# Pooled attention and a routed two-layer network: values products and normalizing of two chunks in halves of heads, an expert index ahead of a fold, one load held for another, and a new table of priorities

## The chip, the cores and the metric

The kernel runs on one core of one Trainium2 chip. The metric is the device time of one execution in microseconds (us), as the median of several runs. Before the change three runs gave 199.23, 200.05 and 202.09 us; their median is 200.05 us.

## What is computed

Eight batches, eight heads, 576 rows, head size 64. Keys and values are averaged over groups of eight rows (72 groups a head), attention runs over these, and its 4608 x 512 output goes through a router that picks one expert of eight for each row and through that expert's two-layer network.

```python
k_p = k.reshape(B, H, Sp, 8, D).mean(axis=3);  v_p = v.reshape(B, H, Sp, 8, D).mean(axis=3)
attn = softmax(scale * q @ k_p.T);             x = (attn @ v_p) as [4608, 512]
expert_idx = argmax(xn @ en.T / tau);          gate_w = softmax(...)[expert_idx]
out[mask_e] = gate_w * (relu(x[mask_e] @ w1[e]) @ w2[e])
```

## The kernel before

The eight batches are eight periods of work that overlap: while TensorE (PE) does the network of batch b, the attention of batch b+1 is put between its products. For each batch the kernel guesses one expert from the mean of the values and loads that expert's two weights; a block behind a branch at the end does a batch again if a row chose another expert.

The kernel is written as named steps, each with an engine, an assumed duration, a priority and the steps it waits for. A planner (`Plan.order`, line 135) runs them once through a model of the engines and the DMA wires, and the order that comes out is the order in which the instructions are written to the engines' queues. Every engine then works its queue strictly in order. The table `TUNED` adds numbers to the priorities, and so sets the order; `LOADS` fixes the order of the loads on GpSimd's queue (POOL); `BEHIND` says which store waits for which load. Where the planner expects PE to be idle in the first part, it writes filler products of ones (`keep_warm`, line 819) into PE's queue; their results are not used.

Names of steps, with the batch as the first number:

- V, K, Q: loads of values, keys and queries (POOL, lines 319 and 325). Batch 0's are cut in two (V0.0, V0.1, K0.0, K0.1, Q0.0, Q0.1). W1b, W2b: the two weights (lines 343 and 349; W10 is the first weight of batch 0). PKb: POOL reads the index of the guessed expert (line 359) and can then issue the weights.
- GM, GC, GL, GD, GE: mean of the values, its copy, its product with the expert embeddings, the maximum and its index on VectorE (DVE, lines 523 and 524), and the one-hot of it.
- VA, VB, KA, KB: folds of values and keys on DVE (line 448 and lines 455, 462); batch 0's keys are summed by PE (line 472). QT: transposes of the queries on DVE (line 548). KT, KE: the keys' transpose on PE and its copy.
- SC, EX: scores on PE (line 589) and exponentials on ScalarE (ACT, line 597), in two halves of the query columns (0 to 269 and 270 to 575 in batch 0), in two-bank PSUM tiles `pa` of which there are two.
- PV, XM, XT, XE, SQ: values product of a chunk of 128 rows (PE, line 634), its division by the row sum (DVE: a reciprocal on line 369 and a product on line 370), its transpose (PE, line 378), the copy of that, the sum of squares. There are five chunks a batch. In batch 0 chunks 0 and 1 need only the first half of the columns and use two PSUM tiles of one bank each, with heads 0 to 3 and 4 to 7.
- H, HE: the first layer in 16 pieces (line 709) and its relu (ACT or DVE, lines 715 and 717). Y, YL, YE, ST: the second layer in four chunks and a last half (lines 721 and 728), its scaling by the gate (line 734 or 736) and the store (SyncE's queue, SP).
- RT, RE, NA to ND: router and gate. PR, PP, PX: the test at the end of whether the branch is taken (lines 867 to 893).

What the diff touches: `store` and `note` (lines 333 to 340), `normalize` (line 364), the loads in `attention` (lines 417 to 436), VA of batch 0 (line 489), the loop over the chunks (lines 625 to 668) and `presence` (line 895 and its call on line 990).

Of the kernel before, what the change touches and what calls it, by code (L numbers as in the profile page):

```python
# [213 lines left out]
def kernel(  # L214
# [24 lines left out]
    NC = 5  # L239
# [854 lines left out]
```

## Time and profile before

| | |
|---|---|
| median of 3 runs | 200.05 us (199.23 to 202.09) |
| the profiled execution | 200.91 us |
| its span, first to last instruction | 199.1 us |
| PE busy | 188.6 us (95%), of this 15.7 us filler products |
| DVE, ACT, POOL busy | 139.8, 136.3, 43.0 us |
| mean granted TensorE clock | 0.993 |
| moved by DMA | 38.71 MB, mean 194 GB/s |

The profile is of one execution. Busy time of PE is from the start of a product to its modelled end, and consecutive products overlap; so PE can be shown busy where it is slowed by something else. POOL's rows for DMA are the time of issuing, the landing is counted separately.

### The profile page before, as it was taken

Reading aid. Unit: us, or ns where it says so; the run is one execution under the profiler, and the core shown is the slowest. Engines: PE = TensorE matmul, PEld = TensorE weight load, DVE = VectorE, ACT = ScalarE, POOL = GpSimd, SP = SyncE. Lnnn points to the kernel's source line nnn. Section 1 sums busy time; section 2 is a strip of 40 time slices with the busy share of each in tenths; the row PEclk is TensorE's granted clock in tenths of the full one; section 3 lists DMA queues with packets and bytes.
Section 4 is the critical chain, followed back from the end, with each engine's and each line's share of the span. In section 5 each row is a group of like instructions: output and inputs, shape, how many; then the busy total and the mean of one; then the engine's idle time right before and its main releaser. Section 6 shows DMA issues by size and latency. Waiting matters only on the chain.

```text
span 199.1 us, 5342 instructions
## 1 busy us (share of the span) xinstructions
PE 188.6 (95%) x2080; PEld 123.8 (62%) x2081; DVE 139.8 (70%) x409; ACT 136.3 (68%) x313; POOL 43.0 (22%) x59
## 2 busy tenths in 40 slices
PE   7969999999999999999999999999999999999980
PEld 5754787547864676468666566567665677568540
DVE  1274799659996996678997997878998559322610
ACT  4017886768896979759966779459976988558440
POOL 7443025232204321025102500043000510002000
PEclk9999999999999999999999999999999999999997
DMA  3999999999999999999999999999996699992042
GB/s 46 185 197 185 206 210 192 205 193 205 212 182 189 215 208 201 213 206 232 246 172 214 186 233 247 215 204 230 254 219 199 182 213 212 233 317 71 3 176 71
DMA packets 27839, 38.71 MB, mean 194 GB/s; under 512 B 4248, under 2 KB 14488, under 8 KB 27808
## 3 DMA queue, kind: packets, MB, share of 16 engines
q0 software_dynamic: 21904, 28.85, 86.7%
q1 hardware_dynamic: 5824, 9.39, 13.9%
q8 instruction: 18, 0.29, 0.6%
q14 instruction: 13, 0.11, 0.2%
q10 hardware_dynamic: 80, 0.07, 0.1%
HBM read 61.88 MB, written 9.44 MB: 358 GB/s over the span
## 4 chain that ended last, share of the span: by engine, by line
PE 80%; DVE 8%; DMA 4%; issue 2%; ACT 1%; POOL 1%; DVEq 0%; ACTq 0%; POOLq 0%
PE pb L709 27%; PE pb L721 22%; PE pa L589 6%; PE pa L709 5%; DMA kr<-in_k_dram 4%; PE pa L721 3%; DVE x L370 3%; PE pa L634 3%; PE pb L378 3%; PE pb L821 2%; PE pb L728 2%; PE pb L387 2%; DVE r_all L369 1%; DVE qT L548 1%; PE pb L472 1%
## 5 line engine op out<-in xcount | busy, mean ns | idle before, releaser
L709 PE MATMUL pb<-xt,w 128*128 128x288 f16 (+2 forms) x432 | 61.3, 287 | 0.0
L709 PEld LDWEIGHTS <-w 128*128 128x128 f16 x512 | 47.1, 98 | 15.1 <-issue 4.6
L721 PE MATMUL pb<-w,hT 128*128 128x512 f16 x224 | 52.7, 379 | 0.0
L597 ACT ACTIVATE at<-pa 72x576 f16<-72x576 f32 (+2 forms) x64 | 38.2, 642 | 3.9 <-PE pa L589 3.5
L721 PEld LDWEIGHTS <-hT 128*128 128x128 f16 x256 | 23.2, 98 | 24.9 <-issue 1.3
L655 ACT ACTIVATE sq<-x 128x512 f16<-128x512 f16 x40 | 25.2, 631 | 13.8 <-DVE x L370 8.8
L715 ACT ACTIVATE hT<-pb 128x288 f16<-128x288 f32 (+2 forms) x74 | 28.6, 411 | 5.4 <-PE pb L709 3.3
L734 ACT ACTIVATE y<-pb,gm_all 128x512 f32<-128x512 f32 (+1 forms) x29 | 18.5, 639 | 14.0 <-PE pb L721 10.9
L370 DVE TENSOR_TENSOR x<-pa,r_all 128x512 f16<-128x512 f32 x38 | 26.3, 692 | 2.1
L548 DVE STREAM_TRANSPOSE qT<-qq 128x576 f16<-128x576 f16 x32 | 23.2, 754 | 0.4 <-DMA qq<-in_q_dram 0.4
L398 POOL TENSOR_TENSOR ssq_all<-ssq_all,half_c 128x5 f32<-128x5 f32 x8 | 10.4, 1294 | 50.8 <-ACT sq L655 50.8
L349 POOL DMA_DIRECT2D w<-in_moe_w_dram x8 | 5.5, 688 | 64.3 <-PE pb L728 17.0
L717 DVE TENSOR_SCALAR hT<-pb 128x288 f16<-128x288 f32 (+2 forms) x34 | 14.8, 447 | 6.5 <-PE pb L709 6.2
L448 DVE TENSOR_TENSOR vr<-vr 72x2048 f16<-72x2048 f16 (+1 forms) x16 | 15.1, 941 | 3.3 <-DMA vr<-in_v_dram 3.3
L821 PE MATMUL pb<-ones_m 128*128 128x256 f16 x102 | 15.7, 297 | 1.5 <-DVE half_c L828 1.5
L589 PE MATMUL pa<-qT,kpT 32*72 32x288 f16 (+2 forms) x256 | 15.6, 294 | 0.0
L378 PEld LDWEIGHTS <-x 128*128 128x128 f16 x160 | 10.9, 98 | 6.3 <-DVE x L370 2.3
L378 PE MATMUL pb<-ident_h,x 128*128 128x128 f16 x144 | 13.7, 220 | 1.0 <-DVE x L370 0.7
L634 PEld LDWEIGHTS <-at 72*128 72x128 f16 x320 | 13.1, 98 | 1.9 <-issue 0.3
L634 PE MATMUL pa<-vpx,at 72*128 72x65 f16 x304 | 14.2, 194 | 0.0
L448 DVE TENSOR_TENSOR kr<-kr 72x2048 f16<-72x2048 f16 (+1 forms) x14 | 13.2, 942 | 0.3 <-DMA kr<-in_k_dram 0.3
L650 ACT COPY xt<-pb 128x512 f16<-128x512 f16 (+1 forms) x25 | 13.0, 538 | 0.5 <-PE pb L378 0.3
(116 smaller groups left out, 197.1 us busy)
## 6 DMA issues: line engine op xcount, KB each, us to landing
w<-in_moe_w_dram POOLq DMA_DIRECT2D x16, 1024.0 KB, 16.5
out_dram<-y SPq DMA_DIRECT2D x32, 256.0 KB, 5.9
vr<-in_v_dram POOLq DMA_DIRECT2D x7, 576.0 KB, 21.0
kr<-in_k_dram POOLq DMA_DIRECT2D x7, 576.0 KB, 17.6
qq<-in_q_dram POOLq DMA_DIRECT2D x7, 576.0 KB, 16.0
out_dram<-y SPq DMA_DIRECT2D x15, 64.0 KB, 7.0
qq<-in_q_dram POOLq DMA_DIRECT2D x2, 288.0 KB, 8.9
vr<-in_v_dram POOLq DMA_DIRECT2D x1, 512.0 KB
```

Of the source, the lines that this page charges most:

```text
L370: nc.vector.tensor_tensor(out=x[:, ts(i, np_)], in0=pxv[:, :, 1:129].rearrange("p a (r d) -> p a r d", d=D), in1=rv.unsqueeze(3).to_broadc ...
L378: nc.tensor.transpose(out=pt.bitcast(FP16)[:, ts(w, 128)], in_=xf[:, ts(w, 128)], identity=ident_h)
L448: nc.vector.tensor_tensor(out=t[:, :, 0:m], in0=t[:, :, 0:m], in1=t[:, :, m:2 * m], op=ALU.add)
L548: nc.vector.transpose(out=qT.tile[:, a].rearrange("p t c e -> p (t c e)")[:, cols], in_=qq.tile[:, a, cols]),
L589: nc.tensor.matmul(out=tiles[m // 2].tile[0:gs, m % 2 * 512:m % 2 * 512 + (p1 - p0) * T], lhsT=kpT.tile[ts(m, R), a, c, 0:gs], rhs=qT.tile ...
L597: nc.scalar.activation(out=t.tile[:, :, p0 * T:p1 * T].rearrange("g r (p t) -> g r p t", t=T), in_=p.tile[0:G].rearrange("g (r c) -> g r c ...
L634: nc.tensor.matmul(out=px[h // 2 // np_].tile[:, o:o + 65], lhsT=at[h // 2].tile[:, h % 2, c0:c0 + 128], rhs=vp.tile[:, h // 2, 1 + h % 2 ...
L655: nc.scalar.activation(out=sq, in_=x.tile.rearrange("p a r d -> p (a r d)"), func=AF.Square, accum_out=ssq_all[:, b, c:c + 1])
L709: nc.tensor.matmul(out=p[:, 0:c1 - c0], lhsT=w1v[:, kk, w // 2, w % 2, :], rhs=xt[:, kk, c0:c1], start=(kk == 0), stop=(kk == 3))
L715: nc.scalar.activation(out=dst, in_=src, func=AF.Relu)
L721: landing[f"Y{c}"] = nc.tensor.matmul(out=p, lhsT=hT[w][:, ts(c, 128)], rhs=w2[:, w // 2, w % 2, :], start=(w == 0), stop=(w == 7))
L821: nc.tensor.matmul(out=p[:, 256:512], lhsT=ones_m[:, 0:128], rhs=ones_m[:, 0:256], start=True, stop=True)
```

## The change

1. `LOADS` is reordered. On POOL's queue V1 is no longer issued right behind Q0.1, it comes behind PK0, and it waits in addition until K0.1 has landed (`wait_for`). K2 goes ahead of PK1, V2 behind it, and the later loads are reordered too. The planner's assumed delays of K0.1 and Q0 change.
2. In batch 0 the fold VA waits for GD (the index) and no longer for GC, so the index is written ahead of the fold on DVE.
3. In chunks 0 and 1 of batch 0 PV and XM are two steps each, one for each half of the heads (names PV0.0.0, PV0.0.1 and so on). A half waits only for the exponentials of its own heads. The instructions are the same in number: before, the step already issued one reciprocal and one product for each of the two PSUM tiles.
4. `presence` gets a later base for its priority.
5. `TUNED` is another table, so the order of nearly everything differs. PE's queue has 114 fillers, 103 before; the other instructions are the same in kind and number on every engine, but for one relu more on ACT and one fewer on DVE.

```diff
 TUNED = {
-    "GM5": 79.1, "Y1.0": 28.3, "RT7": 37.3, "SC6.1.1": -29.8, "VA7": 104.9, "H3.4.0": -54.3,
...
+    "Y2.3": 90, "YL4": 232.5, "PV5.2": -222.7, "PV1.3": 117.9, "H6.5.1": 29.6, "H0.4.1":
...
 LOADS = """
-V0.0 V0.1 K0.0 K0.1 Q0.0 Q0.1 V1 PK0 W10 K1 Q1.0 W20 V2 PK1 W11 K2 Q2.0 V3 W21 V4 K3 PK2 W12
...
+V0.0 V0.1 K0.0 K0.1 Q0.0 Q0.1 PK0 V1 W10 K1 Q1.0 W20 K2 PK1 V2 W11 Q2.0 V3 W21 PK2 W12 K3
...
+    def wait_for(ins, name):
+        tc.add_manual_dep(ins, landing[name], mybir.DependencyInfo(
+            mybir.DependencyClass.Sync, mybir.DependencyReason.DATA), reason="late transfer")
+
     def note(name, load):
         landing[name] = load.ins.name
+        if name == "V1":
+            wait_for(load.ins, "K0.1")
...
-                    uses=[raw], mode=(8, 1.25 if c == "V" else 0.3, 1.2), late=0.9)
+                    lambda c=c, src=src, raw=raw: note(n(c, 1), load_rows(src, b, raw.tile, 64)),
+                    uses=[raw], mode=(8, 1.25 if c == "V" else 0.6, 1.2),
+                    late=0.9 if c == "V" else 1.6)
...
         add(n("VA"), 'DVE', 1.14, pr(-0.5), lambda: halve(vr.tile, 4),
-            [n("V"), "XM0.4" if b == 1 else None] if b else [n("GC")], uses=[vr], late=0.1)
+            [n("V"), "XM0.4" if b == 1 else None] if b else [n("GD")], uses=[vr], late=0.1)
...
-            add(n("PV", c), 'PE', 0.27, pr(f), pv,
-                [n("EX", i, j) for i in range(1 if c < 2 else 2) for j in range(HP)] + [n("VB")],
-                takes=px, uses=at + [vp], late=0.22)
-            add(n("XM", c), 'DVE', 0.84 if len(px) == 1 else 1.1, pr(f), norm, [n("PV", c)],
-                takes=[x], uses=px,
-                late=0.12)
+            done = []
+            for i, p in enumerate(px):
+                nh = H // len(px)
+                m = (i,) if len(px) > 1 else ()
+                add(n("PV", c, *m), 'PE', 0.27 / len(px), pr(f),
+                    lambda i=i, nh=nh, pv=pv: pv(range(i * nh, (i + 1) * nh)),
+                    [n("EX", q, j) for q in range(1 if c < 2 else 2)
+                     for j in range(i * nh // 2, (i + 1) * nh // 2)] + [n("VB")],
+                    takes=[p], uses=at[i * nh // 2:(i + 1) * nh // 2] + [vp], late=0.22)
+                done.append(add(n("XM", c, *m), 'DVE', 0.84 if len(px) == 1 else 0.55, pr(f),
+                                lambda i=i, norm=norm, p=p, n_=len(px): norm(i, n_, px=[p]),
+                                [n("PV", c, *m)], takes=[] if i else [x],
+                                uses=[p] + ([x] if i else []), late=0.12))
...
-    presence(B * PERIOD - 200.0)
+    presence(B * PERIOD - 60.0)
```

On POOL's queue, from batch 0's queries (`qq`) to the first load of the second layer's weights, it stood so before (`vr_78` is V1, `kr_76` K1, `w_67` W10, `w_71` W20, `vr_77` V2; line 359 is PK0):

```order
L325 DMA qq_79<-in_q_dram 128x1152 x2
L319 DMA vr_78<-in_v_dram 72x8x512
L359 TENSOR_LOAD ix_all
L359 ISA x2
L343 ISA
L343 DMA w_67<-in_moe_w_dram 128x4x1024
L319 DMA kr_76<-in_k_dram 72x8x512
L325 DMA qq_80<-in_q_dram 128x2x1152
L349 ISA
L349 DMA w_71<-in_moe_w_dram 128x4x1024
L319 DMA vr_77<-in_v_dram 72x8x512
```

And it stands so now:

```order
L320 DMA qq_79<-in_q_dram 128x1152 x2
L359 TENSOR_LOAD ix_all
L359 ISA x2
L314 DMA vr_78<-in_v_dram 72x8x512
L343 ISA
L343 DMA w_67<-in_moe_w_dram 128x4x1024
L314 DMA kr_76<-in_k_dram 72x8x512
L320 DMA qq_80<-in_q_dram 128x2x1152
L349 ISA
L349 DMA w_71<-in_moe_w_dram 128x4x1024
L314 DMA kr_75<-in_k_dram 72x8x512
```

V1 has moved behind the reading of the index, and the load behind W20 is K2 (`kr_75`) where it was V2.

On DVE's queue, from the copy of the values' mean (`mv`) to the transposes of batch 0's queries (`qT_81`), it stood so before (`vr_77` is folded, `vpx_87` is the folded values, `kpT_85` the transposed keys):

```order
L537 CAST mv_126<-pb_63 128x4
L448 TENSOR_TENSOR vr_77<-vr_77 72x8x256
L523 MAX mx_all<-pb_63 128x8
L524 MAX_INDEX ix_all<-mx_all,pb_63 128x8
L448 TENSOR_TENSOR vr_77<-vr_77 72x8x128
L462 TENSOR_TENSOR vpx_87<-vr_77 72x4x128
L548 STREAM_TRANSPOSE qT_81<-qq_79 128x576
L568 COPY kpT_85<-pb_65 128x2x72
L548 STREAM_TRANSPOSE qT_81<-qq_79 128x576
```

And it stands so now:

```order
L538 CAST mv_126<-pb_63 128x4
L524 MAX mx_all<-pb_63 128x8
L525 MAX_INDEX ix_all<-mx_all,pb_63 128x8
L449 TENSOR_TENSOR vr_77<-vr_77 72x8x256
L549 STREAM_TRANSPOSE qT_81<-qq_79 128x576
L449 TENSOR_TENSOR vr_77<-vr_77 72x8x128
L463 TENSOR_TENSOR vpx_87<-vr_77 72x4x128
L549 STREAM_TRANSPOSE qT_81<-qq_79 128x576
L569 COPY kpT_85<-pb_65 128x2x72 x2
```

The index stands ahead of the whole fold, the first transpose stands inside the fold, and both copies of the keys stand behind the second transpose.

On ACT's queue, at the end of batch 0's first layer, it stood so before (`hT` are relus of pieces of 320 columns, `at` are batch 1's exponentials, `lg_all` is batch 0's gate):

```order
L715 ACTIVATE hT_102<-pb_65 128x320
L715 ACTIVATE hT_103<-pb_63 128x320
L597 ACTIVATE at_93<-pa_62 72x2x288
L597 ACTIVATE at_94<-pa_61 72x2x288
L715 ACTIVATE hT_104<-pb_64 128x320
L700 ACTIVATE lg_all<-lg_all,lnxs 128x40
```

And it stands so now:

```order
L726 ACTIVATE hT_105<-pb_65 128x320
L726 ACTIVATE hT_101<-pb_63 128x320
L726 ACTIVATE hT_98<-pb_64 128x320
L598 ACTIVATE at_93<-pa_61 72x2x288
L598 ACTIVATE at_94<-pa_62 72x2x288
L711 ACTIVATE lg_all<-lg_all,lnxs 128x40
```

All relus of batch 0 now stand ahead of the first exponentials of batch 1.

## Rows read from the trace of the kernel before

**Rows 1.** Windows: PE, PEld, DVE, ACT, POOL busy us (instructions), PE clock, DMA share, GB/s.
```profile
36.83:193.31 156.48, 155.49 (x1682) 100.30 (x1679) 116.60 (x336) 116.22 (x268) 28.11 (x33) 1.00 1.04 203
```

**Rows 2.** Waits of PEld from 36.83 to 193.31 us: total us, times, longest.
```profile
PEld L378 <- DVE x L370: 1.7, 6, 0.4
PEld L518 <- DVE mv L537: 0.8, 2, 0.5
```

**Rows 3.** Timeline of PE, 9 to 26 us: start, us, what [idle before].
```profile
9.94 0.25 PE L518 MATMUL pb<-enT,mv 128*128 128x8 f16 x4
...
11.92 1.92 PE L472 MATMUL pb<-kr,ident_h 72*128 72x256 f16 x16 [1.06 <-DMA kr<-in_k_dram]
...
14.99 0.82 PE L821 MATMUL pb<-ones_m 128*128 128x256 f16 x6
15.74 0.43 PE L589 MATMUL pa<-qT,kpT 32*128 32x270 f16 x8
...
25.43 1.04 PE L709 MATMUL pb<-xt,w 128*128 128x256 f16 x8
```

**Rows 4.** Timeline of PE, 34 to 37 us.
```profile
34.08 0.44 PE L589 MATMUL pa<-qT,kpT 32*72 32x288 f16 x8
...
35.76 0.47 PE L589 MATMUL pa<-qT,kpT 32*72 32x288 f16 x8
36.16 0.83 PE L821 MATMUL pb<-ones_m 128*128 128x256 f16 x6
36.83 1.89 PE L721 MATMUL pb<-w,hT 128*128 128x512 f16 x8
```

**Rows 5.** Timeline of DVE, 10 to 14 us: index, fold, first query transpose.
```profile
10.93 0.16 DVE L523 MAX8 mx_all<-pb 128x8 f32<-128x8 f32 x1
...
11.21 0.17 DVE L524 FIND_INDEX8 ix_all<-mx_all,pb 128x8 uint32<-128x8 f32 x1
11.29 0.67 DVE L448 TENSOR_TENSOR vr<-vr 72x1024 f16<-72x1024 f16 x1
11.99 0.42 DVE L462 TENSOR_TENSOR vpx<-vr 72x512 f16<-72x512 f16 x1
12.78 0.78 DVE L548 STREAM_TRANSPOSE qT<-qq 128x576 f16<-128x576 f16 x1 [0.36 <-DMA qq<-in_q_dram]
```

**Rows 6.** Timeline of POOL: issues of V0, V1, W10, W20.
```profile
1.56 1.47 POOL L319 DMA_DIRECT2D vr<-in_v_dram  x2 [0.85 <-POOLq L1075]
...
6.33 0.89 POOL L319 DMA_DIRECT2D vr<-in_v_dram  x1
12.92 0.79 POOL L343 DMA_DIRECT2D w<-in_moe_w_dram  x1 [5.70 <-DVE vpx L462]
...
15.26 0.79 POOL L349 DMA_DIRECT2D w<-in_moe_w_dram  x1
```

**Rows 7.** DMA issues of V0.1, V1, W20: KB, us to landing.
```profile
vr<-in_v_dram POOLq DMA_DIRECT2D x1, 64.0 KB, 5.8
vr<-in_v_dram POOLq DMA_DIRECT2D x1, 576.0 KB, 11.6
w<-in_moe_w_dram POOLq DMA_DIRECT2D x1, 1024.0 KB, 20.5
```

**Rows 8.** Timeline of ACT: batch 0's exponentials; batch 1's first, and a relu.
```profile
16.20 5.32 ACT L597 ACTIVATE at<-pa 72x540 f16<-72x540 f32 x8 [1.69 <-PE pa L589]
...
34.56 1.18 ACT L597 ACTIVATE at<-pa 72x576 f16<-72x576 f32 x2
35.64 0.43 ACT L715 ACTIVATE hT<-pb 128x320 f16<-128x320 f32 x1
```

**Rows 9.** Timeline of DVE, 39 to 45 us: batch 2's fold and batch 1's first normalizing.
```profile
39.12 1.94 DVE L448 TENSOR_TENSOR vr<-vr 72x2048 f16<-72x2048 f16 x2 [1.59 <-DMA vr<-in_v_dram]
...
43.49 0.21 DVE L369 RECIPROCAL r_all<-pa 128x8 f32<-128x8 f32 x1 [1.97 <-PE pb L505]
43.73 0.69 DVE L370 TENSOR_TENSOR x<-pa,r_all 128x512 f16<-128x512 f32 x1
```

More of the change, by code (lines that the diff above doesn't have):

```diff
@@ L338, in store @@
         if name in behind:
-            tc.add_manual_dep(st.ins, landing[behind[name]], mybir.DependencyInfo(
-                mybir.DependencyClass.Sync, mybir.DependencyReason.DATA), reason="late store")
+            wait_for(st.ins, behind[name])
     def load_w1(e_val, w1, cond=None):
@@ L427, in attention @@
                     lambda c=c, src=src, raw=raw: note(n(c), load_rows(src, b, raw.tile)),
-                    takes=[raw], mode=wire(ROWS_DMA), tail=tails.get(n(c), 0.0), late=0.9)
+                    ["K0.1"] if n(c) == "V1" else [], takes=[raw], mode=wire(ROWS_DMA), tail=tails.get(n(c), 0.0), late=0.9)
         if b == 0:
@@ L431, in attention @@
                 add(n("Q", i), 'POOL', 0.8, at_load(n("Q", i)), lambda i=i: load_q(b, qq, i, 1),
-                    takes=[] if i else [qq], uses=[qq] if i else [], mode=(16, 1.3 + i, 1.2), late=0.9)
+                    takes=[] if i else [qq], uses=[qq] if i else [], mode=(16, 1.3 + i, 1.2), late=-0.2 if i else 0.1)
         else:
@@ L618, in attention @@
                             after, takes=[p], uses=[qT, kpT], late=0.22, mode='r32')
-                    add(n("EX", half, 2 * a + i), 'ACT', 0.56, pr(f),
+                    add(n("EX", half, 2 * a + i), 'ACT', 0.56 if b or not half else 0.6, pr(f),
                         lambda half=half, t=t, p=p: expo(half, t, p),
                         [n("SC", half, a) if b else n("SC", half, a, i)],
-                        takes=[] if half else [t], uses=[p] + ([t] if half else []), late=0.12)
+                        takes=[] if half else [t], uses=[p] + ([t] if half else []),
+                        late=0.12 if b else 0.18)
         for c in range(NC):
@@ L628, in attention, with pv @@
             np_ = HP // len(px)
-            def pv(c=c, px=px, np_=np_):
+            def pv(heads, c=c, px=px, np_=np_):
                 c0 = c * 128 if c < 4 else S - 128
-                for h in range(H):
+                for h in heads:
                     o = h // 2 % np_ * 256 + h % 2 * 65
@@ L638, in pv, with norm @@
                         start=True, stop=True)
-            def norm(c=c, px=px, x=x):
-                normalize([p.tile for p in px], r_all[:, b, c], x.tile)
+            def norm(i, n_, c=c, px=px, x=x):
+                nh = HP // n_
+                normalize([p.tile for p in px], r_all[:, b, c, 2 * i * nh:2 * (i + 1) * nh],
+                          x.tile[:, ts(i, nh)])
             def xtr(c=c, x=x, pt=pt):
@@ L658, in attention @@
             f = 0.5 + 0.08 * c
-            add(n("PV", c), 'PE', 0.27, pr(f), pv,
-                [n("EX", i, j) for i in range(1 if c < 2 else 2) for j in range(HP)] + [n("VB")],
-                takes=px, uses=at + [vp], late=0.22)
-            add(n("XM", c), 'DVE', 0.84 if len(px) == 1 else 1.1, pr(f), norm, [n("PV", c)],
-                takes=[x], uses=px,
-                late=0.12)
-            add(n("XT", c), 'PE', 0.23, pr(f), xtr, [n("XM", c)], takes=[pt], uses=[x], late=0.22)
+            done = []
[11 more added lines that the diff above has]
+                                uses=[p] + ([x] if i else []), late=0.12))
+            add(n("XT", c), 'PE', 0.23, pr(f), xtr, done, takes=[pt], uses=[x], late=0.22)
             add(n("XE", c), ('DVE', 'ACT'), (0.34, 0.56) if c < 4 else (0.22, 0.36), pr(f), xcopy, [n("XT", c)],
                 takes=[] if c else [xt], uses=[pt] + ([xt] if c else []), late=0.1)
-            add(n("SQ", c), 'ACT', 0.63, pr(f + 0.2), square, [n("XM", c)], uses=[x], late=0.12)
+            add(n("SQ", c), 'ACT', 0.63, pr(f + 0.2), square, done, uses=[x], late=0.12)
         pl = Buf(bank, psum)
@@ L896, in presence @@
         p, last = Buf(bank, psum), [f"RE{b}" for b in range(B)] + [f"GE{b}" for b in range(B)]
-        add("PR", 'DVE', 1.0, base, in_range, [f"XM{b}.{c}" for b in range(B) for c in range(NC)],
+        add("PR", 'DVE', 1.0, base, in_range, [s for s in plan.by_name if s.startswith("XM")],
             late=0.1)
```

7 lines of the change are left out of this document (3 added, 4 removed), and 47 rows, old and new, of the table TUNED.

## The prediction

> **What bounds the kernel now.** I read the windows first. From the first product of the second layer (36.83 us) to the end of the last one (193.31 us) PE is shown busy for 155.49 of 156.48 us, at the full clock [rows 1]. A busy PE proves little by itself, since products overlap, so I read next what the weight loads waited for in that stretch: only 1.7 us for the normalized chunks (XM) and 0.8 us for the copy of the mean, 2.5 us together [rows 2]. Waits for DMA are not in that list. So from 36.83 us on the kernel is bound by PE's own work, which the change does not alter: the queue has the same products but for fillers. What can be won there is 2.5 us at most, plus a little at switches between kinds of products.
>
> The rest is the head: 36.83 us in which loads land, batch 0's attention is a chain of four engines, and the first layer of batch 0 begins at 25.43 us [rows 3, 4]. Behind the last product lie 5.8 us (199.1 less 193.31) of scaling, storing and ending; PE's last five products, the last scaling and the last store stand in the same order in both kernels, so I leave the tail as it is.
>
> So the question is whether the first Y of batch 0 comes earlier than 36.83 us, and how many of the 2.5 us stay.
>
> **The index.** MAX8 was written behind the first half of the fold and began at 10.93 us; the products it reads ended at 9.94 + 0.25 = 10.19 us [rows 3, 5]. Ahead of the fold it can begin at about 10.25, so the index is ready at 11.38 - 0.68 = 10.70 us.
>
> **V1 and the load queue.** W10 was issued at 12.92, 1.54 us after the index [rows 5, 6]. With the same distance POOL is free at 12.24 us. Now V1 stands there first. PE's sums of batch 0's keys waited for their load until 11.92 us [rows 3], so K0.1 lands at 11.9 and the hold ends before POOL can issue V1 anyway: it costs nothing. It also gains nothing: V1 was queued behind K0 and Q0 before, and the loads landed in the order of issue. But the queue now runs dry behind Q0. From rows: V0, on an empty queue, was issued at 1.56 and its second part, issued about 2.4, landed 5.8 us later, at 8.2, so 6.7 us after the first issue [rows 6, 7]. V1 issued at 12.24 would land at 18.9, against 6.33 + 11.6 = 17.9 before: 1.0 us later. The bounds are 0 (the gap is filled by Q0's last packets) and 2.0 (the pick takes longer too); I take 1.0. W10 is issued at 13.1 and no longer matters for the start of H (it comes at about 23.9, before 25.4). W20 landed at 15.26 + 20.5 = 35.8 [rows 6, 7]; the same bytes lie ahead of it, so it lands at 36.8 now.
>
> The Trainium skill (page "DMA: Bandwidth & Descriptors", section "Anatomy of one DMA — SWDGE (gpsimd) path") gives a load a fixed cost of about 2.0 us and bytes over 436 GB/s on top; for V1 that would be an estimate of 3.4 us, and a landing at 15.6, earlier than before. The row of V0 shows 6.7 us for the same size, and I go by the row; by the rule the rival of the late values, below, would lose its ground and the sum would not change.
>
> **The head on DVE, PE and ACT.** The first transpose of the queries waited for Q0.0 until 12.78 [rows 5]; that load is not moved, so it starts there now too. It now stands ahead of the second half of the fold. Behind it come the half fold (0.70 from start to start), the last fold (0.7 with its successor's start), the second transpose (0.75): both copies of the keys come at about 15.4. On PE, the fillers between the keys' transposes and the first scores are 10 instead of 6. They begin at 14.99 and cost (36.83 - 36.16)/6 = 0.11 us each [rows 3, 4], so the first scores start at 14.99 + 1.1 = 16.1 instead of 15.74: later by 0.36. The eight exponentials take 5.32 us without a gap [rows 8], so they end at about 21.9 instead of 21.5. Halving PV and XM of chunks 0 and 1 lets four half products and four half normalizings (about 0.55 us each) go beside the exponentials instead of behind them; their number of instructions does not change, so the halving itself costs nothing. Behind the last exponential there remain the three full chunks on DVE, 0.2 + 0.7 us each [rows 9]: from about 22.5 to 25.2. In the new order all five transposes stand ahead of the first layer, so H waits for the fifth chunk: 25.2 + 0.05 + 0.3 = 25.6 against 25.43 [rows 3]. The gain of the halves (about 0.8 us of DVE behind the exponentials) is given back by the later scores and by waiting for one chunk more.
>
> From there to the first scores of batch 1 it was 34.08 - 25.43 = 8.65 us. In that stretch one transpose (0.22) and five fillers (0.54) are gone, and two more pieces of H of 320 columns (0.55 each) have come in: 8.65 + 0.33 = 9.0, so the scores come at 34.6. The second scores need the PSUM tiles that ACT empties. Before, the exponentials followed the scores at 34.56, and the second scores came at 35.76, with two pieces of H between [rows 4, 8]. Now two relus stand ahead of the exponentials on ACT and no H is left to fill the time: relu of the last piece 0.45 behind 34.6, exponentials 1.18 [rows 8], second scores at 36.3, done 36.7, five fillers 0.54, first Y at 37.3. W20 (36.8) has come by then. So the first Y is later by 37.3 - 36.83 = 0.5 us. Bounds: -0.1 (only W20 limits, 36.8) and +1.3 (W20 at 37.8 and fillers behind it).
>
> **The steady part.** Two fillers have come in (+0.2). Of the 2.5 us of waits [rows 2] I take half away: 1.2. The new order puts single chunks' transposes apart from each other with pieces of H between in batch 1, where before a transpose stood directly behind the values product of the next chunk. Bounds: all 2.5 gone, or 1.5 us more than before (three more of the longest single wait, 0.5). The changed places of the later loads I take at nothing, since no wait of PE for a load is in the list [rows 2]; but the DMA engines are as busy as PE there, a share of 1.04 [rows 1], so a load that comes late finds no slack to catch up in, and that is the ground of the third case below. `presence` has the same place behind the first Y of the last batch, and costs nothing.
>
> **The sum.** On the profiled execution: 200.91 + 0.5 + 0.2 - 1.2 = 200.4. That execution stands 0.86 us above the median of 200.05; on the median the same terms give 199.55, I say 199.5 us. A measurement of this kernel can tell about 2% (4 us) from no change, and this is within it.
>
> **Rivals.**
>
> *The waits go* (chance 0.25). The scores of batch 1 do not delay the first Y (the lower bound above, -0.1) and the order clears all 2.5 us: 200.05 - 0.1 + 0.2 - 2.5 = 197.6. For it speaks that so few places make up the waits; against it that fillers before the first Y have risen from 7 to 16, which a planner writes where it sees PE idle.
>
> *The values come late* (chance 0.25). V2 is issued behind PK1 and lands behind K2: W20 at 36.8 plus 3.4 for K2 and 3.4 for V2 (39.12 less 35.8 was one such load [rows 9]) is 43.6. On DVE the first half of V2's fold now stands ahead of batch 1's first normalizing, whose values product is done at about 44.0 (43.49 before, plus 0.5). DVE takes its queue in order: a V2 that lands after 43.7 delays the first transpose, which PE reaches at about 45.9, by as much (1.25 of fold, 0.9 of normalizing between), and two more chunks behind it. If the dry queue costs 3 us and not 1, V2 lands at 45.6 and PE stands for 1.9 us, no other wait is won: 200.05 + 0.5 + 0.2 + 1.9 = 202.7. Slower than before. It decides from 43.7; my landing is 43.6, so the margin is thin.
>
> *The hold does nothing* is part of the forecast: since K0.1 has landed before POOL can issue V1, taking the hold alone away would change nothing.
>
> **How the numbers follow.** Forecast 199.5 (0.50), the waits go 197.6 (0.25), the values come late 202.7 (0.25). The forecast's own range, by the bounds of its terms, is 198.3 to 201.2. The range of eight in ten takes in the middle of both rivals: 197.1 to 202.8. Faster by over 2% (under 196.0) would need more than all the waits found: 0.07. Slower by over 2% (over 204.1) would need the late values in more than one batch: 0.08. Within: 0.85.
>
> **What would show it.** In the profile of the changed kernel: the index done near 10.7; V1 issued near 12.2 and landing near 18.9; the first scores near 16.1; the first H near 25.6; the first Y near 37.3; from there to the last product 155.5 us. A first Y before 36.5, or a stretch behind it under 154 or over 158 us, makes the forecast wrong; DVE standing for V2 ahead of batch 1's first normalizing would be the third case.

## The result and the profile after

The changed kernel takes 203.05 us (median of 4 runs, 202.69 to 203.77), the kernel before took 199.89 us beside it (4 runs, 199.23 to 202.09). The ratio is 1.0147, 95% interval 1.0098 to 1.0195: slower by 3 us, where 199.5 us was predicted with a range up to 202.8. That is less than the 2% which the prediction took for the least that can be told, but the interval lies clear of 1. The profiled execution took 202.69 us with a span of 200.9 us.

Busy time alone says nothing of this. The page's groups show PE at 189.6 us (94%), 1.0 us more than before. What is new stands in the last column of the groups, idle time and what ended it:

```profile
PE 189.6 (94%) x2091; PEld 125.4 (62%) x2092; DVE 140.9 (70%) x408; ACT 138.0 (69%) x314; POOL 43.0 (21%) x59
...
PE 68%; DMA 13%; DVE 11%; issue 3%; ACT 2%; POOL 2%; POOLq 0%; DVEq 0%
...
L549 DVE STREAM_TRANSPOSE qT<-qq 128x576 f16<-128x576 f16 x32 | 23.0, 752 | 2.9 <-DMA qq<-in_q_dram 2.9
...
L449 DVE TENSOR_TENSOR kr<-kr 72x2048 f16<-72x2048 f16 (+1 forms) x14 | 13.3, 947 | 5.6 <-DMA kr<-in_k_dram 5.5
...
L636 PE MATMUL pa<-vpx,at 72*128 72x65 f16 x304 | 14.3, 194 | 1.8 <-DVE x L370 1.8
```

DVE waits for two kinds of transfers, the first queries (2.9 us) and keys (5.5 us: 2.62 at 41.9 us for batch 2's, behind which PE does not stand, and 2.76 at 151 us for batch 7's), and PE has 1.8 us of waiting for a normalizing (DVE's `x`, line 370) in front of a values product. In the chain of waits (second line) DMA has 13% of the span. The queries, and the keys at 151 us with PE's wait beside them, lead to the two places where the time went, the head and one point late in the steady part.

**The head.** The timelines of DVE, POOL and PE answer to [rows 3 to 6]. DVE first:

```profile
10.28 0.17 DVE L524 MAX8 mx_all<-pb 128x8 f32<-128x8 f32 x1 [0.35 <-PE pb L519]
...
10.57 0.17 DVE L525 FIND_INDEX8 ix_all<-mx_all,pb 128x8 uint32<-128x8 f32 x1
10.65 1.20 DVE L449 TENSOR_TENSOR vr<-vr 72x2048 f16<-72x2048 f16 x1
14.74 0.78 DVE L549 STREAM_TRANSPOSE qT<-qq 128x576 f16<-128x576 f16 x1 [2.89 <-DMA qq<-in_q_dram]
```

POOL's issues of V1, W10 and W20:

```profile
12.19 0.87 POOL L314 DMA_DIRECT2D vr<-in_v_dram  x1 [5.81 <-DMA kr<-in_k_dram]
13.05 0.79 POOL L343 DMA_DIRECT2D w<-in_moe_w_dram  x1
...
15.40 0.77 POOL L349 DMA_DIRECT2D w<-in_moe_w_dram  x1
```

PE: the key sums, the first scores, the first H, batch 1's two scores, the first Y:

```profile
11.94 1.92 PE L473 MATMUL pb<-kr,ident_h 72*128 72x256 f16 x16 [1.03 <-DMA kr<-in_k_dram]
...
17.40 0.43 PE L590 MATMUL pa<-qT,kpT 32*128 32x270 f16 x8 [1.13 <-DVE kpT L569]
...
27.18 0.60 PE L720 MATMUL pb<-xt,w 128*128 128x256 f16 x4
...
36.02 0.47 PE L590 MATMUL pa<-qT,kpT 32*72 32x288 f16 x8
...
37.73 0.44 PE L590 MATMUL pa<-qT,kpT 32*72 32x288 f16 x8
...
38.65 1.67 PE L732 MATMUL pb<-w,hT 128*128 128x512 f16 x7
```

The index and V1's issue come as forecast. The first query transpose comes at 14.74 where it stood at 12.78 [rows 5], and the head shifts behind it: first scores 1.7 us later than in [rows 3], first H 1.75, first Y 1.8 [rows 4].

The windows show the transfer queue at that time (last column GB/s, before it the DMA engines' share). Before:

```profile
13.00:14.00 1.00, 0.84 (x8) 0.50 (x6) 0.55 (x1) 0.12 (x1) 1.00 (x2) 1.00 1.10 172
14.00:15.00 1.00, 0.70 (x10) 0.64 (x11) 0.42 (x2) 0.51 (x2) 1.00 (x2) 1.00 1.47 169
```

After:

```profile
13.00:14.00 1.00, 0.86 (x8) 0.52 (x6) 0.00 (x0) 0.10 (x1) 1.00 (x3) 1.00 0.61 49
14.00:15.00 1.00, 0.68 (x9) 0.62 (x10) 0.26 (x1) 0.54 (x2) 1.00 (x2) 1.00 0.57 62
15.00:16.00 1.00, 1.00 (x14) 0.90 (x11) 1.00 (x2) 0.00 (x0) 1.00 (x2) 1.00 0.85 128
```

From 13 to 15 us the queue moves 49 and 62 GB/s instead of 172 and 169: V1 was issued at 12.19, but the queue is at 128 GB/s again only from 15 to 16. The table of landings gives V1 8.7 us from issue (`vr`, 576 KB), so 20.9 against 17.9 before [rows 6, 7]:

```profile
w<-in_moe_w_dram POOLq DMA_DIRECT2D x2, 1024.0 KB, 17.2
vr<-in_v_dram POOLq DMA_DIRECT2D x1, 576.0 KB, 8.7
```

**The steady part.** From the first Y to the last product it is 157.24 us, where it was 156.49 [rows 1], and the waits of the weight loads for the normalizing have gone from 1.7 to 0.8 us [rows 2]:

```profile
38.65:195.89 157.24, 155.22 (x1684) 100.69 (x1681) 117.34 (x335) 117.82 (x269) 27.67 (x33) 1.00 1.00 202
```

```profile
PEld L378 <- DVE x L370: 0.8, 2, 0.4
```

So small waits were won there, and one large one has come. PE's timeline at 150 us has it, and DVE's has its cause:

```profile
150.85 0.42 PE L636 MATMUL pa<-vpx,at 72*128 72x65 f16 x8
153.11 0.42 PE L636 MATMUL pa<-vpx,at 72*128 72x65 f16 x8 [1.84 <-DVE x L370]
```

```profile
148.00 0.23 DVE L530 TENSOR_SCALAR eb_all<-irow,mx_all 128x8 f32<-128x8 f32 x1
151.00 1.22 DVE L449 TENSOR_TENSOR kr<-kr 72x2048 f16<-72x2048 f16 x1 [2.76 <-DMA kr<-in_k_dram]
152.14 0.20 DVE L369 RECIPROCAL r_all<-pa 128x8 f32<-128x8 f32 x1
152.37 0.69 DVE L370 TENSOR_TENSOR x<-pa,r_all 128x512 f16<-128x512 f32 x1
```

Read the second fence from top to bottom, as DVE does. The third row's input, the values product of chunk 4 of batch 6, was there before 151 us. It stands behind the first step of batch 7's key fold (KA7), and that waits 2.76 us for K7. K7 was issued at 134.50 and took 16.5 us, so it came at 151.0; before, at 130.18 and 17.8 us, so it came at 148.0. Of these 3 us, 1.8 are the later head; counted from the first Y, K7 comes 1.1 us later (112.3 us behind it, 111.2 before). The releaser that the profile names for PE is `DVE x`, a normalizing. The transfer that was late is found only one engine further.

The last product ends at 195.89 us and the execution lasts 5.0 us longer, 5.8 before.

The ratios leave out executions that were disturbed (two of the repeat's 4, four of c_fix's 12, single ones elsewhere), and in the profiled executions of the repeat, c_fix and c_fix_both below the clock stood at half for 6.8 to 10.2 us of the head, so their heads are not read.

### The profile page after: what moved, and what is told of

Read it like the earlier page. It is cut to its first block, busy times and chain, and to the rows that moved or that the text cites. A ratio compares the mean times of both kernels' runs of the same rounds, so it can differ in the third digit from the quotient of the medians.

```text
span 200.9 us, 5365 instructions
## 1 busy us (share of the span) xinstructions
PE 189.6 (94%) x2091; PEld 125.4 (62%) x2092; DVE 140.9 (70%) x408; ACT 138.0 (69%) x314; POOL 43.0 (21%) x59
## 4 chain that ended last, share of the span: by engine, by line
PE 68%; DMA 13%; DVE 11%; issue 3%; ACT 2%; POOL 2%; POOLq 0%; DVEq 0%
PE pb L720 22%; PE pb L732 18%; DMA kr<-in_k_dram 8%; PE pa L590 6%; PE pa L720 5%; DMA qq<-in_q_dram 5%; DVE x L370 4%; PE pa L636 3%; PE pb L378 3%; DVE qT L549 3%; PE pa L732 3%; PE pb L739 2%; PE pb L832 2%; DVE r_all L369 1%; PE pa L739 1%
## 5 line engine op out<-in xcount | busy, mean ns | idle before, releaser
L720 PE MATMUL pb<-xt,w 128*128 128x288 f16 (+2 forms) x416 | 60.1, 286 | 0.0
L720 PEld LDWEIGHTS <-w 128*128 128x128 f16 x512 | 47.3, 98 | 14.5 <-issue 3.9
L732 PE MATMUL pb<-w,hT 128*128 128x512 f16 x232 | 54.8, 379 | 0.0
L726 ACT ACTIVATE hT<-pb 128x288 f16<-128x288 f32 (+2 forms) x74 | 29.4, 409 | 6.7 <-PE pb L720 4.5
L832 PE MATMUL pb<-ones_m 128*128 128x256 f16 x114 | 17.4, 299 | 1.5 <-DVE half_c L839 1.5
L728 DVE TENSOR_SCALAR hT<-pb 128x288 f16<-128x288 f32 x30 | 13.4, 451 | 6.7 <-PE pb L720 6.3
L449 DVE TENSOR_TENSOR kr<-kr 72x2048 f16<-72x2048 f16 (+1 forms) x14 | 13.3, 947 | 5.6 <-DMA kr<-in_k_dram 5.5
L720 PE MATMUL pa<-xt,w 128*128 128x288 f16 (+2 forms) x96 | 15.4, 286 | 0.0
L832 PEld LDWEIGHTS <-ones_m 128*128 128x128 f16 x114 | 11.1, 107 | 4.9 <-issue 1.7
L378 PEld LDWEIGHTS <-x 128*128 128x128 f16 x160 | 10.7, 98 | 4.6 <-DVE x L370 1.7
L314 POOL DMA_DIRECT2D kr<-in_k_dram x9 | 7.3, 807 | 24.3 <-DVE x L370 12.5
(115 smaller groups left out, 199.9 us busy)
## 6 DMA issues: line engine op xcount, KB each, us to landing
vr<-in_v_dram POOLq DMA_DIRECT2D x7, 576.0 KB, 17.8
```

Source lines behind the costliest of these rows:

```text
L449: nc.vector.tensor_tensor(out=t[:, :, 0:m], in0=t[:, :, 0:m], in1=t[:, :, m:2 * m], op=ALU.add)
L720: nc.tensor.matmul(out=p[:, 0:c1 - c0], lhsT=w1v[:, kk, w // 2, w % 2, :], rhs=xt[:, kk, c0:c1], start=(kk == 0), stop=(kk == 3))
L726: nc.scalar.activation(out=dst, in_=src, func=AF.Relu)
L732: landing[f"Y{c}"] = nc.tensor.matmul(out=p, lhsT=hT[w][:, ts(c, 128)], rhs=w2[:, w // 2, w % 2, :], start=(w == 0), stop=(w == 7))
L832: nc.tensor.matmul(out=p[:, 256:512], lhsT=ones_m[:, 0:128], rhs=ones_m[:, 0:256], start=True, stop=True)
```

## The experiments

Each ratio is to the kernel before, run beside it on the same chip. Where a kernel is changed by `move`, the line stands behind `order = plan.order(loads)` and puts one step behind another in the order of writing (`move("V1", "Q0.1")` writes V1 straight behind Q0.1); all else stays.

### Repeated, and the place of V1

The repeat (after_again) is the changed kernel without an edit.

> The changed kernel once more, beside the others of this call. Queue theory (Q0's last packets come late because nothing is queued behind them): the first query transpose starts near 14.7 us again, first Y near 38.7, about 3 us (1.5%) over before. Chance theory (that landing differs from execution to execution): the first transpose starts anywhere between 12.5 and 15, and the time follows it.

Measured: ratio 1.0182 (1.0049 to 1.0315), 1.0147 before. The query transpose began at 14.75 us again.

V1 straight behind the queries and no hold (a_v1_first):

```diff
-        if name == "V1":
-            wait_for(load.ins, "K0.1")
...
+        move("V1", "Q0.1")
```

> The changed kernel with V1 issued right behind Q0.1 again and without the hold; all else in the new order. Queue theory: the first transpose starts near 12.8 and not 14.7, first Y near 37 and not 38.7, time about 1.7 us under the changed kernel (201.3). Chance theory: no systematic difference, 203. If V1 took bandwidth from Q0 (what the hold would be for), the transpose starts later than 14.7.

Measured: 202.17 us, ratio 1.0097 (1.0055 to 1.0139). First transpose at 13.30, first Y at 37.41, with no wait for W20, which landed at 34.49. PE's wait at the key fold is still there (1.86 us), and a stretch at half clock behind it, shown in the last section.

K1 straight behind the queries, V1 still held (a_k1_first: `+ move("K1", "Q0.1")`):

> The changed kernel with K1 issued right behind Q0.1; V1 stays behind the reading of the index and held. Queue theory: any load queued behind Q0 does, the first transpose starts near 12.8, and the queue does not run dry; time about 201.3. Chance theory: 203. If it is V1 itself that matters, the transpose stays at 14.7.

Measured: 203.51 us, ratio 1.0145 (1.005 to 1.0241). First transpose 12.45, first Y 37.75: the head is 0.9 us better than in the changed kernel although V1 is held. What it gained was lost later: PE's wait at the key fold is 2.43 us there, and 3.4 us at half clock follow it.

The other way round, V1 late in the kernel before (b_v1_late: `+ move("V1", "PK0")` there):

> The kernel before with V1 issued behind the reading of the index (no hold); all else in the old order. Queue theory: the first transpose moves from 12.8 to about 14.7 and the scores with it, since the copies of the keys stand between the transposes; first Y from 36.8 to about 38 and the time 1 to 2 us over before. Chance theory: no change of the transpose; the later landing of V1 alone costs under 0.5 us.

Measured: 202.56 us, ratio 1.0107 (1.0024 to 1.0191). The transpose stays at 12.46, against the theory of the queue, and still about 2.1 us are lost (1.0107 of 200 us). PE's timeline shows where:

```profile
35.91 0.83 PE L821 MATMUL pb<-ones_m 128*128 128x256 f16 x6
38.10 1.24 PE L721 MATMUL pb<-w,hT 128*128 128x512 f16 x5 [1.36 <-DMA w<-in_moe_w_dram]
```

W20 landed at 38.05 instead of 35.72, and the first Y waits for it. Its queue stood emptier still, 14 GB/s from 13 to 14 us.

The hold alone (a_no_hold: the two lines with `wait_for` removed, V1 still behind the index pick):

> The changed kernel without the wait for the second key transfer; V1 still stands behind the index pick in GpSimd's queue, so it is issued about 0.6 us earlier (11.6 against 12.19) but still after 11 us. Theory A (what delays the first query transfer is that nothing follows it in the transfer queue while GpSimd stands at a later instruction): the first query transpose stays late, 14.0 to 14.8, and the time stays at 202.5 to 203.5. Theory B (the explicit wait itself disturbs the queue, since the late V1 of the kernel before, without that wait, left the query transpose at 12.5): transpose at 12.4 to 12.9, first layer-two product about 36.9 to 37.3, time about 201.5.

Measured: 202.9 us, ratio 1.0156 (1.0052 to 1.0259); transpose at 14.67. V1 is issued at 12.11 instead of 12.19 (11.6 was expected), so the explicit wait does nothing that can be measured: it is V1's place behind the pick that makes it late.

The first query transpose behind the values' fold (a_qt_behind: `+ move("QT0.0.0", "VB0")`):

> The changed kernel with the first query transpose behind the second half of the values' fold and the copy of the ones' column on VectorE (1.06 us of work that stood behind it and now runs while the query transfer is late). Theory (the late transfer itself sets the transpose; the work queued behind it adds to the loss): the transpose still begins at 14.7, the second one at 15.4 instead of 16.46, first scores at 16.5 instead of 17.40, first layer-two product about 37.8, time 0.7 to 0.9 us under the changed kernel. Rival (the first scores wait for keys and not for these): first scores unmoved, no gain.

Measured: ratio 1.0105 (0.9989 to 1.022), which decides nothing. In its profiled execution the queries landed at 13.22, so there was no late transfer to hide work behind. The first scores came at 16.17, but the first Y waited 1.48 us for W20 (landed 39.03) and came at 39.07.

### The key fold at 151 us

KA7 behind a normalizing (a_kfold_behind: `+ move("KA7", "XM6.2")`).

> The changed kernel with one step moved on VectorE: the first half of batch 7's key fold stands behind the first normalizing of batch 6 that it stood ahead of. Theory (the fold waits for K7's landing and holds the normalizing that is queued behind it): the 1.8 us wait of TensorE at about 151 us is gone, the time from the first layer-two product to the last is 155.2 to 155.8 us instead of 157.2, and the kernel takes 2 us less than the changed kernel, about 201. The head is as in the changed kernel (first query transpose 14.7, first layer-two product 38.6). Rival (TensorE loses the same time at the next thing it has to wait for, the folded keys of batch 7): the wait comes back at the scores of batch 7 and the total stays within 0.5 us of 203.

Measured: 201.19 us, ratio 1.0062 (1.0021 to 1.0102). PE's wait is gone and the stretch is 155.43 us. The head was not as expected: the first transpose came at 12.53, and PE waited 1.13 us for W20. XM6.2, however, is the third of the normalizings there, and KA7 was moved past the second step of its own fold too: batch 7's keys are pooled over four rows of eight, and DVE's chain from K7 to batch 7's scores is 1.2 us shorter than it may be. The same holds for a_fix, a_fix_qt, a_k1_kfold and a_fix_whole. Their heads are read as they are; what the fold costs is taken from c_kfold and c_fix, where nothing is left out.

The load instead of the fold (a_k7_early: `+ move("K7", "V7")`):

> The changed kernel with one transfer moved: K7 is issued ahead of the second layer-one weights of batch 5 and of batch 6's index pick, straight behind V7; VectorE's order is the changed kernel's. Theory (TensorE's wait at 151 us is K7 landing late for a fold that stands ahead of a normalizing, so an earlier landing cures it as well as a later fold): K7 lands before 148 us, the fold does not wait, stretch from the first to the last layer-two product 155.2 to 156.0 us, time about 201, like the kernel with the fold moved. Rival (the fold itself, 1.9 us of VectorE in front of the normalizing, makes the wait whether or not it is late): a wait of 0.5 to 1.5 us stays there. What may come instead: the weights pushed back by K7's 576 KB land 2.9 us later and TensorE waits for them.

Measured: 205.77 us, ratio 1.0268 (1.0223 to 1.0313). The fold begins at 148.16 without a wait, and PE waits longer than ever for W25, the second layer's weights of batch 5, which K7 now precedes:

```profile
147.05 0.25 PE L519 MATMUL pb<-enT,mv 128*128 128x8 f16 x4
150.26 1.02 PE L732 MATMUL pb<-w,hT 128*128 128x512 f16 x4 [2.95 <-DMA w<-in_moe_w_dram]
```

So K7 came earlier at the price of another transfer; from 122 to 150 us the DMA engines' share is 1.09 to 1.15 in the changed kernel, and the one exchange that was tried gained nothing. Whether a fold that is on time would still hold the normalizing is not tested by it, since the wait for W25 comes first. The place of the fold is what was changed next.

KA7 one place later, behind chunk 4's normalizing and ahead of its second step (c_kfold: `+ move("KA7", "XM6.4")`):

> The changed kernel with the first step of batch 7's key fold one place later on VectorE: behind the one normalizing (chunk 4 of batch 6) that it stood directly ahead of, and still ahead of the fold's second step and of the other two normalizings. Theory (TensorE's 1.8 us wait at 151 us is that one normalizing standing behind a transfer): the wait there goes, stretch 155.3 to 156.2 us, time about 201.2, as with the longer move. Rival (the wait only moves: the next normalizing now stands behind the fold, and TensorE's transpose of that chunk or of batch 7's keys waits instead): a wait of 0.5 to 1.5 us at 153 to 156 us, time 202 to 202.7.

Measured: 201.3 us, ratio 1.0059 (1.0028 to 1.009). The same 1.8 us less than the changed kernel. DVE's timeline, and PE's beside it:

```profile
149.33 0.21 DVE L369 RECIPROCAL r_all<-pa 128x8 f32<-128x8 f32 x1 [1.16 <-PE pa L636]
...
150.69 1.94 DVE L449 TENSOR_TENSOR kr<-kr 72x2048 f16<-72x2048 f16 x2 [0.43 <-DMA kr<-in_k_dram]
152.67 0.49 DVE L456 TENSOR_TENSOR kp<-kr 72x256 f16<-72x256 f16 x2
153.08 0.20 DVE L369 RECIPROCAL r_all<-pa 128x8 f32<-128x8 f32 x1
```

```profile
151.31 0.39 PE L378 MATMUL pb<-ident_h,x 128*128 128x128 f16 x4
151.53 1.89 PE L732 MATMUL pb<-w,hT 128*128 128x512 f16 x8
153.26 0.30 PE L560 MATMUL pb<-ident_h,kp 72*128 72x72 f16 x4
...
155.12 0.39 PE L378 MATMUL pb<-ident_h,x 128*128 128x128 f16 x4
```

K7 lands no earlier than the fold needs it, but only one normalizing had to come first: the two others find PE busy with Y. The window over the stretch:

```profile
38.20:193.97 155.77, 155.37 (x1682) 100.54 (x1681) 116.88 (x330) 116.62 (x267) 27.60 (x33) 1.00 1.01 204
```

### Parts together

V1 straight behind the queries, no hold, KA7 moved too far as above (a_fix: `+ move("V1", "Q0.1")`, `+ move("KA7", "XM6.2")`):

> Two moves in the changed kernel: V1 is issued straight behind the queries without a wait (as in the kernel before), and the first half of batch 7's key fold stands behind batch 6's normalizing. Theory (the loss is the sum of the dry transfer queue in the head and the late key fold): first layer-two product at 37.4 as with V1 first alone, stretch to the last one 155.2 to 156, no half clock at 152 to 156 us, time 199.2 to 200.2, so no slower than the kernel before. Rival (there is a third loss that these two hide): 201 or more.

Measured: 199.22 us, ratio 0.9962 (0.9929 to 0.9996). First transpose 12.25, first Y 36.64, stretch 155.23.

The same with the query transpose behind the fold as well (a_fix_qt: `+ move("QT0.0.0", "VB0")`):

> The kernel with V1 straight behind the queries and batch 7's key fold behind the normalizing, and also the first query transpose behind the second half of the values' fold and its copy. Theory (with the queue full the query transfer lands at 12.3 to 13.3, and 1.06 us of work fits in front of it): first scores 0.3 to 1.0 us earlier, but the first layer-two product waits for weights that land at their own time, so the total gains at most 0.5 us: 198.7 to 199.3, 0.3 to 0.7% under the kernel before. Rival (the head is bound by these transposes): 0.8 us gained, 198.4.

Measured: 199.64 us, ratio 0.9953 (0.9929 to 0.9978): no difference that can be told from a_fix. The first scores came at 15.51 and the first Y at 36.76.

V1 held, K1 in its place, KA7 moved (a_k1_kfold: `+ move("K1", "Q0.1")`, `+ move("KA7", "XM6.2")`):

> The changed kernel with V1 still held until the second key transfer has landed, but with K1 straight behind the queries so that the queue has work while V1 is held; the key fold of batch 7 stands behind the normalizing. Theory (holding V1 costs through the empty queue, not through V1): no wait for layer-two weights, first layer-two product at 37.4 to 37.9 (the layer-one weights land about 0.8 us after they are wanted, as K1's bytes go ahead of them), stretch 155.2 to 155.8, time 200.0 to 200.6. Rival (V1 itself has to be early): first layer-two product after 38.2 and 201 or more, as with the fold moved alone (201.19).

Measured: 200.34 us, ratio 0.9988 (0.9961 to 1.0014). First Y at 37.63 with no wait for W20; the first H waited 0.57 us for W10, which landed at 26.1 behind K1's bytes. V1 landed at 21.2, as late as in the changed kernel, and did no harm. So what costs is not V1 but the empty queue.

The halves of heads undone in a_fix (a_fix_whole):

```diff
-            for i, p in enumerate(px):
...
+            add(n("PV", c), 'PE', 0.27, pr(f), lambda pv=pv: pv(range(H)),
...
+            done = [add(n("XM", c), 'DVE', 0.84 if len(px) == 1 else 1.1, pr(f),
```

> The kernel with V1 straight behind the queries and batch 7's key fold behind the normalizing, with the halves of heads undone: chunks 0 and 1 of batch 0 have one values product and one normalizing again, each waiting for all heads (the planner then writes the work up to the first layer of batch 1 in another order; what follows is as it was). Theory (the halves bring nothing that lasts: first scores to first H took 9.69 us before the change and 9.78 with it): first H 9.7 to 10.2 us behind the first scores, first layer-two product no later than 37.2, stretch from there 155.2 to 156, time 199.3 to 200.3 against 199.2 with the halves. Rival (the halves take about 0.8 us of VectorE out of the chain in front of H): first H 10.5 us or more behind the first scores, first layer-two product after 37.3, time over 200.

Measured: 199.9 us, ratio 0.9982 (0.9951 to 1.0012). From first scores to first H it is 9.54 us, 9.78 with the halves (a_fix): they win nothing that shows there. Its profiled execution holds something else, the late queries, although V1 stands behind them:

```profile
14.56 0.78 DVE L547 STREAM_TRANSPOSE qT<-qq 128x576 f16<-128x576 f16 x1 [2.70 <-DMA qq<-in_q_dram]
```

Its first Y came at 38.51. The order of the work around the halves changes with this edit too.

The whole repair with nothing left out (c_fix: no hold, `+ move("V1", "Q0.1")`, `+ move("KA7", "XM6.4")`):

> V1 straight behind the queries without a wait, and the fold's first step behind chunk 4's normalizing as in c_kfold, nothing left out. Theory: first layer-two product at 36.6 to 37.4 (38.5 where the query transfer comes late), stretch 155.3 to 156.2, time 199.2 to 200.2, no slower than the kernel before and 3 us under the changed kernel. Rival (wait moves): 200.3 to 201.

Measured: ratio 1.0005 (0.9971 to 1.0039), stretch 155.65 us: the time of the kernel before, not better.

The whole fold behind all three normalizings (c_fix_both: `+ move("KA7", "XM6.2")`, `+ move("KB7", "KA7")`):

> As c_fix, but both steps of batch 7's key fold stand behind all three normalizings of batch 6. If the normalizings behind the fold still cost, this is faster than c_fix by what is left there (up to 1 us); if the fold's end is what TensorE wants next (the transpose of batch 7's keys), this is slower than c_fix by up to 1.4 us. Theory (there is work enough between): the same as c_fix within 0.4 us, 199.2 to 200.2.

Measured: ratio 1.0134 (1.0084 to 1.0183). Now the fold is too late, and the transpose of batch 7's keys waits for it:

```profile
157.58 0.44 PE L558 MATMUL pb<-ident_h,kp 72*128 72x72 f16 x4 [2.09 <-DVE kp L454]
```

One place earlier than in c_kfold the fold costs PE 1.8 us through the normalizing behind it; with the whole fold two normalizings later the keys are late by 2.1 us.

### What the heads show together

Profiled executions, times in us, sorted by what stood behind the queries in the transfer queue ("empty" means that nothing did until the index was read). In a_fix_qt and a_qt_behind the first transpose was itself moved. Left out are the three heads at half clock; a_no_hold had half clock for 3.4 us from 14.6.

| kernel | queue behind the queries | first query transpose | W20 landed | PE waits for W20 | first Y |
|---|---|---|---|---|---|
| before | V1 | 12.78 | 35.72 | no | 36.83 |
| a_v1_first | V1 | 13.30 | 34.49 | no | 37.41 |
| a_fix | V1 | 12.25 | 34.62 | no | 36.64 |
| a_fix_qt | V1 | 12.93 | 34.81 | no | 36.76 |
| a_fix_whole | V1 | 14.56 | 34.51 | no | 38.51 |
| a_k1_first | K1 | 12.45 | 33.89 | no | 37.75 |
| a_k1_kfold | K1 | 12.39 | 34.79 | no | 37.63 |
| after | empty | 14.74 | 37.04 | no | 38.65 |
| a_no_hold | empty | 14.67 | 36.83 | no | 39.10 |
| b_v1_late | empty | 12.46 | 38.05 | 1.36 | 38.10 |
| a_kfold_behind | empty | 12.53 | 38.24 | 1.13 | 38.29 |
| a_qt_behind | empty | 13.52 | 39.03 | 1.48 | 39.07 |
| a_k7_early | empty | 12.33 | 38.34 | 1.55 | 38.38 |
| c_kfold | empty | 12.38 | 38.16 | 1.14 | 38.20 |

Two things are mixed here. The queries land late, at 14.5 or after, in some executions with either queue; what decides that is open. It shows earlier, and with either place of V1: where the first transpose came at 13.3 or later, the first part of batch 0's keys, issued at 3.0, had landed at 11.2 to 11.7, in all others at 10.6 to 11.0. Where they are on time, an empty queue makes W20 land at 38.05 to 39.03 instead of 33.89 to 35.72, and the first Y comes at 38.1 to 39.1 instead of 36.6 to 37.8. Where they are late, the first Y is at 38.5 to 38.7 with either queue (a_fix_whole, after). So holding V1 costs about 1.4 us in an execution whose queries come on time (38.20 of c_kfold less 36.83 of before), and next to nothing in the one pair seen of the others.

## Why the prediction was wrong

**What held.** The index at 10.7 us (10.73), POOL free for V1 at 12.24 (12.19), the hold without effect of its own (a_no_hold: 1.0156 against 1.0147). From first H to first Y 11.7 us were reckoned, and 11.47 came, hardly more than the 11.40 before. The steady part was reckoned at 156.49 + 0.2 - 1.2 = 155.5 us; with the one large wait taken out it is 155.77 (c_kfold) and 155.65 (c_fix). Of the 2.5 us of small waits (for normalizings and for the copy of the mean) 1.2 were to be won; c_kfold has 1.8 left and c_fix 1.2, so 0.7 to 1.3 were.

**The step that failed in the steady part:** "The changed places of the later loads I take at nothing, since no wait of PE for a load is in the list". The list named PE's releasers, and a load that DVE waits for does not stand there. The place of KA7 ahead of a normalizing, with a K7 that lands 3 us later (1.1 of them not by the later head), cost 1.8 us: 1.0147 less 1.0059 is 0.9% of 200 us. The mechanism was in the prediction as the rival of the late values, a fold in front of a normalizing in DVE's order, but at V2 and batch 1, and at a time of 202.7. There the changed kernel's profile shows no wait: V2 landed at 44.27, after the 43.7 named, but batch 1's chain was late as well, and the normalizing followed the fold's first half at 45.45. In c_kfold, with its queries on time, V2 landed at 44.34 and the rival may have come in small; from 38.2 to 60 us its weight loads wait 0.7 us for normalizings, and those of the changed kernel and of c_fix not at all:

```profile
PEld L378 <- DVE x L370: 0.7, 2, 0.5
```

That the rival's time, 202.7, lies next to the 203.05 measured is luck: it reckoned a head 0.5 us later and one wait of 1.9 us at batch 1, where the profile has a head 1.8 us later and 1.8 us at batch 7. The same thing had to be looked for at every fold of the new order, against the new place of its load in the queue. The trace of before showed what margin there was: its fold of K7 waited 0.28 us for its transfer and had two normalizings ahead of it:

```profile
147.07 0.69 DVE L370 TENSOR_TENSOR x<-pa,r_all 128x512 f16<-128x512 f32 x1
148.05 1.22 DVE L448 TENSOR_TENSOR kr<-kr 72x2048 f16<-72x2048 f16 x1 [0.28 <-DMA kr<-in_k_dram]
```

**The step that failed in the head:** "V1 issued at 12.24 would land at 18.9 ... W20 ... lands at 36.8 now". V1 took 8.7 us from issue in the changed kernel and 7.1 in a_kfold_behind and b_v1_late, where 6.7 was reckoned: that is near. But W20 landed not 1.0 but 1.3 us later than before in the profiled execution (37.04), and 2.3 to 3.3 us later in executions with queries on time. The windows from 13 to 20 and from 20 to 34 us say how much the queue lost, and when. Before:

```profile
13.00:20.00 7.00, 6.50 (x64) 3.25 (x62) 3.21 (x8) 4.30 (x8) 3.88 (x5) 1.00 1.13 181
20.00:34.00 14.00, 13.57 (x176) 10.68 (x174) 12.38 (x35) 10.61 (x28) 3.11 (x4) 1.00 1.16 207
```

After:

```profile
13.00:20.00 7.00, 5.36 (x60) 3.35 (x60) 4.39 (x11) 2.74 (x6) 4.01 (x6) 1.00 0.88 130
20.00:34.00 14.00, 13.89 (x155) 9.98 (x155) 11.24 (x32) 11.09 (x28) 2.87 (x3) 1.00 1.15 208
```

The 51 GB/s that are missing over 7 us are 0.36 MB, an estimate of 1.7 us at 208 GB/s; by the same windows c_kfold (133 against a_fix's 190) loses 1.9 us and b_v1_late (110) 2.4. From 20 us on the rate is that of before, so the loss neither grows nor is made up. It is larger than the 1.0 us that the prediction read off V0's and V1's landings; why W20 came 0.4 us less late than that in the changed kernel, and 1.6 us more in c_kfold (38.16 against a_fix's 34.62), is open. The empty queue's price was a term of the sum, with bounds of 0 and 2.0, and it was sized too small; the first Y was put at 37.3 and is at 38.2 or later. By the rule of the Trainium skill (page "DMA: Bandwidth & Descriptors", section "Anatomy of one DMA — SWDGE (gpsimd) path") that the prediction set beside it, V1 would have come at 15.6, by an estimate of 3.4 us from issue. The trace does not agree: 7.1 us is the least that was measured for V1 on the empty queue.

"That load is not moved, so it starts there now too", of the first queries, failed in the profiled execution: 14.74 instead of 12.78. The change is not shown to be the cause, since a_fix_whole has it with a full queue and c_kfold has not with an empty one. Neither of the two profiled executions in the old order has it, five of the fifteen in the new one do, which is too few to say that the order plays no part. It stood in the way of reading the profile, because this late landing hid the wait for W20 that five of the seven readable executions with the empty queue have.

**The range.** The bounds of the terms, all at their upper end, give 200.05 + 1.3 + 0.2 + 1.5 = 203.05 us, and at their lower end 197.65. "The forecast's own range, by the bounds of its terms, is 198.3 to 201.2" is narrower, and no step says how it was narrowed.

**The sum as the runs have it.** Changed kernel 1.0147; KA7 one place later 1.0059; V1 back behind the queries in addition 1.0005. That is 1.8 us for the fold and 1.1 us for the empty queue (the last two intervals overlap a little; with KA7 too far, 1.0062 and 0.9962 are apart). What the new order wins in the steady part, 0.8 us by the profiled executions, is not seen in the ratio of c_fix, whose interval reaches 0.6 us below the kernel before. The halves and the earlier index gave nothing that was seen: the index is 0.64 us earlier, but the first Y waits for transfers and the attention's chain, not for it. The index's place was not undone by itself. That a_fix lies 0.4% under the kernel before comes with the shortened fold and is no gain.

## What to carry to other kernels

A change in the order of loads has to be followed to the engine that consumes each load, and there to what is queued behind the consumer: an engine that works in order hands a late transfer on to work that does not need it, and the profile then names that work as the releaser. Holding a transfer back wins nothing when the queue has nothing else to do: if one must wait, another belongs in its place. Before a table of priorities is judged, its one or two large waits should be taken out by hand: here one place cost 1.8 us, more than all the small waits that the table won.

## What had not been expected

The same landing, that of batch 0's first queries, came between 12.2 and 14.7 us in profiled executions of kernels with the same transfers up to there, so one trace of a head is not enough to judge an edit by.

A wait of PE of about 2 us can be followed by more. In a_v1_first the same wait for KA7 stood at 150.0 to 151.9 us, and behind it the granted clock was at half (column behind POOL's):

```profile
152.00:153.00 1.00, 1.00 (x15) 0.61 (x14) 0.96 (x4) 0.95 (x3) 0.00 (x0) 0.82 1.15 217
153.00:154.00 1.00, 1.00 (x4) 0.42 (x3) 0.93 (x4) 0.10 (x1) 0.00 (x0) 0.50 1.06 246
154.00:155.00 1.00, 1.00 (x4) 0.30 (x2) 0.65 (x1) 0.62 (x2) 0.00 (x0) 0.50 1.09 268
155.00:156.00 1.00, 1.00 (x7) 0.54 (x6) 0.00 (x0) 0.23 (x1) 0.00 (x0) 0.50 1.11 264
```

Its stretch is 158.94 us, 1.7 more than that of the changed kernel, which has the same wait at full clock. By the mean granted clock five of its ten executions look like this one (0.986 to 0.989, 202.4 to 203.9 us) and five do not (0.996 to 0.999, 201.3 to 201.9 us), so its ratio of 1.0097 holds some of it. The profiled executions of a_k1_first and c_fix_both show such 3.4 us as well, those of a_no_hold, a_qt_behind and a_k7_early do not behind waits of 1.5 to 3.0 us. So in one profiled execution a wait of 1.86 us cost nearly twice its length, and whether it does changes from one execution to the next; what decides it is open.
